# Fewer and larger VectorE instructions around a windowed attention, softmax in PSUM, and one more pair of product tiles added by VectorE

## Chip, cores and metric

One core of one Trainium2 chip. The metric is device time in microseconds of one execution; the time before is the median of three runs.

## The reference

The result mixes a windowed attention `a` and a gated MLP `b` by a gate `g` per row. S = 2048 rows, D = 1024, 32 heads of 32, MLP width 3584. In shortened form:

```python
g = sigmoid((x * gate_w).sum(-1, keepdims=True))
q, k, v = split_heads(x @ wqkv)              # 32 heads of 32
idx = pos[:, None] - arange(8) * 2           # a window of 8 keys, 2 apart
logits = einsum("hsd,hswd->hsw", q, k[idx]) * 32 ** -0.5   # -1e9 where idx < 0
a = einsum("hsw,hswd->hsd", softmax(logits), v[idx]) @ wo
b = (gelu(x @ w_gate) * (x @ w_up)) @ w_down
out = g * a + (1 - g) * b
```

## The kernel before

All data are bf16, sums are in f32 in PSUM. One large SBUF tile, `arena`, holds nearly everything; the constants `R_...` are offsets in KB per partition, and the same place serves several stages in turn. Every large matrix product is done in a Strassen-Winograd form: seven products of halves in place of eight, with sums of weight blocks and of row blocks made beforehand by VectorE.

**The loop.** `x` (transposed) is kept as forms R11 ... T4 for two halves of 1024 rows (s = 0, 1). A `Unit` is two blocks of 128 output columns for one half of the rows: 28 matmuls of 128x128 by 512 (L355), in seven products p1 to p7. Units are q-k tiles (each gives 128 columns of q and the same of k), v tiles, and gate and up tiles of the MLP. The program walks them in the loop at L1342; this text calls one turn of it a **slot**. In slot b the order on TensorE is: p1 of unit b, p73 of unit b-1 (products S3 and S4), p5, then reductions if any are due, p2 and p6 of unit b, p4 of unit b-1. After p73 VectorE does the **join** of unit b-1 (L401): it adds the p5 part to two PSUM banks. p4 of unit b-1 writes one of these banks again. There are 78 units in the walk (slots 2 to 77): 16 q-k, 8 v, and from slot 26 on gate and up.

**The planner.** All other VectorE work is put behind the joins by a planner at build time. It is a list of generators (`bg(gen, prio, wake)`); each yields the cost that it declares for the instruction that it has just issued. `run_bg` is called once at the end of each slot with a credit of 4.7 or 4.8 us (more where reductions were issued) and steps the awake task of the lowest priority number until under 0.3 of the credit is left. `due(n, t)` finishes a task at the start of slot n at the latest. So the declared costs and the credit fix the order of VectorE's instructions, and every engine then runs its own queue in order.

The tasks that matter here:
- `qk_prods` (priority 2): for each q-k tile three products of q with eight shifted copies of k (256 columns each, the fourth block of 256 goes to DRAM for later), as one instruction of 4,096 elements per partition and one of 2,048 (L603 and L596), or three of 2,048. Six product tiles are used in turn, three per q-k tile. For two pairs of tiles (`ADDED`) `qk_add` adds the second tile's products to the first's (L641).
- `qk_reduce` on TensorE (L608): for each product tile four matmuls with a pattern of ones sum over the head's columns, into banks 5 to 7. A pair takes 24 matmuls, an added pair 12.
- `softmax` and `softmax_back`: mask, maximum (L713), subtraction (L715), then the exponential on ScalarE (L723) in a later slot, then sum (L730), reciprocal, gate, and the product into `attn_all` (L735). The exponent's argument `ee` is an f32 area of `arena`, one per call (`R_EX`). From there the weights go to DRAM.
- `spill` (priority 4): the same for the fourth blocks, read back from DRAM; `spill_reduce` uses banks 5 and 6.
- `pv_all` (priority 4.2, then 5): loads weights and v, products (L772) and three levels of folds (L778) for eight blocks. Its last block ends near the end of the loop; its work area lies where the buffer A22 of the down projection will be.
- `sums_pair` (priority 1): four sums of weight blocks per pair of MLP column blocks (L315), one slot after `load_pair` (L170, two DMAs of 512 KB on SP) and before the pair's first unit.
- `h_task` (priority 0): product of gelu(gate) and up (L246), for the last pairs also a scaling with 1 - g (L249), and the store to DRAM by POOL. That of the last pair for s = 0 has priority 5.5 and may run in the slot in which it is made.
- `scale_task`: scalings of loaded h with 1 - g (L943); one of them has priority 6 and runs at the end of the loop.
- `gate_task` (priority 0): the gate's sum, tanh and copies through DRAM, a step per slot.

**Down projection.** `run_last` ends the loop; `down(0)` and `down(1)` follow. They use ten buffers in the arena for h blocks (A11, A12, A21, A22), weights and forms. `pre_down_2` and `pre_down_3` issue the loads of A22, A21, A12 and R21 on SP, in this order; `pre_down_4` has POOL load the last two blocks of A11, A12, A21 and A22 once h's last store for s = 0 has landed. In `down(0)` A11 x R11 and A12 x R21 are plain (L1104); four other products are done in a second Strassen-Winograd level (`level2`, L1071), seven products each, with left and right forms made by VectorE (`forms_L` L1029, `forms_R` L1037) from sums of the buffers (`comb_task` L952).

Of the kernel before, what the change touches and what calls it, by code (L numbers as in the profile page):

```python
# [9 lines left out]
ALU = mybir.AluOpType  # L10
# [26 lines left out]
R_EX = (194.5, 81, 50, 81, 84)  # L37
R_MD = 72
R_ATTN = 73
# [3 lines left out]
R_PROD = 84  # L43
# [25 lines left out]
def kernel(  # L69
# [68 lines left out]
    with tc.manual_schedule(engines={mybir.EngineType.PE, mybir.EngineType.DVE, mybir.EngineType.Activation,  # L138
# [18 lines left out]
        raw = [reg4(R_RAW[i], 2, KT, 2 * P) for i in range(2)]  # L157
        sums = [reg(R_S[i], 4 * 2 * HK * P).rearrange("p (f m k n) -> p f m k n", f=4, m=2, k=HK) for i in range(2)]
# [8 lines left out]
        def load_pair(dst, i):  # L167
            for m, src in ((0, B_w_gate), (1, B_w_up)):
                if i > 1:
                    nc.sync.dma_start(out=dst[:, m, :, :],  # L170
                                      in_=src[:, 2 * P * i:2 * P * (i + 1)].rearrange("(k p) n -> p k n", p=P))
                    continue
                for a in range(2):
                    c0 = (2 * a + i) * P
                    nc.sync.dma_start(out=dst[:, m, :, a * P:(a + 1) * P],
                                      in_=src[:, c0:c0 + P].rearrange("(k p) n -> p k n", p=P))
# [34 lines left out]
        def x_form3(s):  # L211
            f = xf[s]
            TT(out=flat(f.T3), in0=flat(f.R22), in1=flat(f.R12), op=ALU.subtract)
# [70 lines left out]
        def gate_task(s):  # L284
            ts = slice(s * SUP, (s + 1) * SUP)
            zc = small.tile([P, HK, ZI], F32, tag="zc", bufs=2)
            zs = small.tile([P, ZI], F32, tag="zs", bufs=2)
            go = small.tile([P, 2, ZI], BF16, tag="go", bufs=2)
            yield None
            nc.gpsimd.dma_start(out=zc[:], in_=z_d[:, ts].rearrange("g (p i) -> p g i", i=ZI))  # L290
            yield None
            V.tensor_reduce(out=zs[:], in_=zc[:].rearrange("p g i -> p i g"), axis=AX.X, op=ALU.add)
            nc.scalar.activation(out=zs[:], in_=zs[:], func=ACT.Tanh, scale=0.5)
            yield 0.15
            yield None
# [12 lines left out]
            gated.add(s)  # L308

        def sums_pair(w, sm):  # L310
            L11, L12 = w[:, :, 0:HK, 0:P], w[:, :, HK:KT, 0:P]
            L21, L22 = w[:, :, 0:HK, P:2 * P], w[:, :, HK:KT, P:2 * P]
            for o_, a, b_, op in ((sm[:, 0], L21, L22, ALU.add), (sm[:, 1], sm[:, 0], L11, ALU.subtract),
                                  (sm[:, 2], L11, L21, ALU.subtract), (sm[:, 3], L12, sm[:, 1], ALU.subtract)):
                TT(out=o_, in0=a, in1=b_, op=op)  # L315
                yield 0.64

        def gu_forms(w, sm, m):
            r = lambda k0, a: (lambda kt: w[:, m, k0 + kt, a * P:(a + 1) * P])
            z = lambda n: (lambda kt: sm[:, n, m, kt, :])  # L320
            return {"L11": r(0, 0), "L12": r(HK, 0), "L22": r(HK, 1), "S1": z(0), "S2": z(1), "S3": z(2), "S4": z(3)}

        def sums_first(m):
            (L11, L12), (L21, L22) = ((r[:, m, 0:HK, :], r[:, m, HK:KT, :]) for r in raw_ab)
            sm = sums_gu[m]
            for o_, a, b_, op in ((sm[:, 0], L21, L22, ALU.add), (sm[:, 1], sm[:, 0], L11, ALU.subtract),
                                  (sm[:, 2], L11, L21, ALU.subtract), (sm[:, 3], L12, sm[:, 1], ALU.subtract)):
                TT(out=o_, in0=a, in1=b_, op=op)
                yield 0.64
# [124 lines left out]
        def sums_qk(part):  # L454
            L11, L12, L21, L22 = wq
            S1, S2, S4 = sq
            for o_, a, b_, op in (((S1, L21, L22, ALU.add), (S2, S1, L11, ALU.subtract)),
                                  ((L21, L11, L21, ALU.subtract), (S4, L12, S2, ALU.subtract)))[part]:
# [79 lines left out]
        def sums_v():  # L538
            L11, L12 = wv4[:, 0:HK, :, 0:4], wv4[:, HK:KT, :, 0:4]
            L21, L22 = wv4[:, 0:HK, :, 4:8], wv4[:, HK:KT, :, 4:8]  # L540
            for o_, a, b_, op in ((sv[0], L21, L22, ALU.add), (sv[1], sv[0], L11, ALU.subtract),
                                  (sv[2], L12, sv[1], ALU.subtract), (L21, L11, L21, ALU.subtract)):
# [32 lines left out]
        pr_off = [R_PR, R_PR + 4, R_PROD, R_PR + 8, R_PR + 12, R_PROD + 4]  # L575
# [19 lines left out]
        def qk_mult(dst, q, k):  # L595
            TT(out=dst, in0=q.rearrange("p (o s) -> p o s", o=1).to_broadcast([P, NWIN, AC]),  # L596
               in1=_win_ap(k, [[-DIL, NWIN], [1, AC]]), op=ALU.mult)

# [3 lines left out]
        def qk_mult2(dst, q, k, sq, sk):  # L602
            TT(out=dst, in0=_win_ap(q, [[sq, 2], [0, NWIN], [1, AC]]),  # L603
               in1=_win_ap(k, [[sk, 2], [-DIL, NWIN], [1, AC]]), op=ALU.mult)
# [7 lines left out]
        ADDED = {(1, 1), (1, 7)}  # L612
# [3 lines left out]
        def qk_prods(u, s, t):  # L616
# [44 lines left out]
        SPILL = ((((R_PR, R_PR + 4), (R_PR + 8, R_PR + 12)), ((R_PR + 8, R_PR + 12), (R_PROD, R_PROD + 4))),  # L661
                 (((R_PROD, R_PROD + 4), (R_PR + 4, R_PR + 12)), ((R_PR + 4, R_PR + 12), (R_PR, R_PR + 8))))

        def spill(s):
# [3 lines left out]
            for g, (x, y) in enumerate(SPILL[s]):  # L668
                for i, ef in enumerate((x, y)):
                    t = QG * g + 2 * i  # L670
                    if credit[0] > 1.5:
                        qk_mult2(pair_at(*ef), qb[s][:, t, :], kb[s][:, t, HALO:HALO + AC], AC, KV)
                        yield 2.21
                        continue
                    for j in range(2):
                        qk_mult(reg3(ef[j], NWIN, AC), qb[s][:, t + j, :], kb[s][:, t + j, HALO:HALO + AC])
# [24 lines left out]
        def softmax(a, cnt, b0, e):  # L701
            ee = regf(R_EX[e], cnt * SC)
            e4 = ee.rearrange("p (a w s) -> p a w s", a=cnt, w=NWIN)
            sw = ee.rearrange("p (a w s) -> p a s w", a=cnt, w=NWIN)
            lg = banks[:, b0:b0 + cnt, :]
# [568 lines left out]
        def head():  # L1274
            xs, f = xf[0], []
            for i, o in enumerate((R_PROD, R_ATTN)):
# [39 lines left out]
            T(xs.T3, xs.R22, xs.R12)  # L1316
# [83 lines left out]
```

## Time and profile before

| what | us |
|---|---|
| median of the runs (715.04 to 715.99) | 715.1 |
| the profiled execution, its own time | 715.41 |
| its span, first to last instruction | 713.6 |
| TensorE busy | 704.6 |
| VectorE busy | 675.4 |
| ScalarE busy | 329.8 |

The span is 1.8 us shorter than the execution's own time. TensorE's clock was granted at 0.999. The page's first block gives the busy time of each engine (PE is TensorE's matmuls, PEld its weight loads, DVE is VectorE, ACT ScalarE, POOL GpSimd, SP SyncE); its fourth block follows back from the last instruction what released what. In the timeline a line has start, length, engine, source line, operation, output and input, the count of merged instructions, and in brackets the idle time before it with what ended it. The waits view has total, number and longest of the waits in us.

### The profile page before, as it was taken

The page shows a single profiled execution, that of the slowest core. Times are in us where ns is not written, and L with a number is a line of the kernel's source. Part 1 is how long each engine was busy: PE and PEld are TensorE (multiplying, and loading weights), DVE is VectorE, ACT ScalarE, POOL GpSimd, SP SyncE. Part 2 cuts the span into 40 slices and gives each one's busy share as a digit, 9 for nine tenths or more (in the row PEclk, how much of TensorE's full clock was granted, in tenths as well). Part 3 has the DMA queues.
Part 4 walks back from the last instruction along what each step waited for, and adds up shares of the span by engine and source line. Part 5 has one row for each costly group of instructions (what it writes and reads, how often), then busy time and mean ns, then how long its engine had stood idle before and what let it go on. Part 6 is the DMA issues. An engine that isn't in the chain of part 4 may idle for free.

```text
span 713.6 us, 10641 instructions
## 1 busy us (share of the span) xinstructions
PE 704.6 (99%) x4021; PEld 407.4 (57%) x4077; DVE 675.4 (95%) x641; ACT 329.8 (46%) x602; POOL 143.6 (20%) x248
## 2 busy tenths in 40 slices
PE   9999999999999999999999999999999999999998
PEld 4466666655544444444444444444447886758887
DVE  3999999999999999999999999999789999899997
ACT  5554445445557665555555555555322321132431
POOL 1243444115502432221210100101110002100011
PEclk9999999999999999999999999999999999999999
DMA  9989454283375768575662764372981799995951
GB/s 296 326 227 274 153 183 151 85 216 126 118 244 186 234 200 270 163 242 180 216 181 95 273 209 164 114 269 64 393 347 39 305 402 400 421 427 219 386 227 60
DMA packets 94755, 162.03 MB, mean 227 GB/s; under 512 B 23680, under 2 KB 71200, under 8 KB 90352
## 3 DMA queue, kind: packets, MB, share of 16 engines
q1 hardware_dynamic: 77632, 105.46, 43.0%
q0 software_dynamic: 16352, 48.29, 20.0%
q10 hardware_dynamic: 720, 7.60, 2.7%
q8 instruction: 32, 0.52, 0.3%
q14 instruction: 19, 0.16, 0.1%
HBM read 112.17 MB, written 54.14 MB: 233 GB/s over the span
## 4 chain that ended last, share of the span: by engine, by line
PE 96%; DVE 2%; DMA 1%; issue 1%; SPq 0%; ACT 0%; DVEq 0%
PE banks L355 67%; PE banks L1071 19%; PE banks L1104 9%; PE banks L608 2%; DMA arena<-in_B_w_gate_dram 1%; DVE arena L401 0%; DVE arena L943 0%; PE banks L274 0%; DVE arena L772 0%; DVE arena L1285 0%; DVE arena L246 0%; DVE arena L249 0%; DVE arena L223 0%; SPq L144 0%; ACT arena L363 0%
## 5 line engine op out<-in xcount | busy, mean ns | idle before, releaser
L355 PE MATMUL banks<-arena 128*128 128x512 bf16 x2191 | 484.7, 379 | 4.2 <-DVE arena L401 0.9
L355 PEld LDWEIGHTS <-arena 128*128 128x128 bf16 x2240 | 245.7, 110 | 241.4 <-issue 7.7
L1071 PE MATMUL banks<-arena 128*128 128x256 bf16 x1260 | 138.3, 273 | 0.0
L1071 PEld LDWEIGHTS <-arena 128*128 128x128 bf16 x1260 | 123.3, 98 | 15.2 <-issue 0.3
L382 ACT COPY arena<-banks 128x512 f32<-128x512 f32 x80 | 46.9, 586 | 129.7 <-PE banks L355 129.7
L401 DVE TENSOR_TENSOR arena<-banks,arena 128x1024 bf16<-128x1024 f32 x80 | 97.4, 1219 | 4.7 <-PE banks L355 4.0
L363 ACT CAST arena<-banks 128x512 bf16<-128x512 f32 x104 | 60.8, 585 | 42.4 <-PE banks L355 41.1
L772 DVE TENSOR_TENSOR arena<-arena 128x2048 bf16<-128x2048 bf16 (+1 forms) x45 | 74.1, 1670 | 0.4
L778 DVE TENSOR_TENSOR arena<-arena 128x2048 bf16<-128x2048 bf16 (+2 forms) x54 | 68.1, 1261 | 1.0
L252 POOL DMA_DIRECT2D h_d<-arena x28 | 20.3, 730 | 232.8 <-DVE arena L246 154.5
L1104 PE MATMUL banks<-arena 128*128 128x512 bf16 x281 | 62.4, 379 | 0.4
L390 ACT COPY banks<-banks 128x512 f32<-128x512 f32 x80 | 45.6, 570 | 22.3 <-PE banks L355 20.7
L1029 DVE TENSOR_TENSOR arena<-arena 128x2304 bf16<-128x2304 bf16 x40 | 53.3, 1353 | 0.5
L377 ACT COPY banks<-banks 128x512 f32<-128x512 f32 x80 | 46.1, 576 | 14.4 <-PE banks L355 13.3
L1076 ACT COPY banks<-banks 128x256 f32<-128x256 f32 x60 | 21.4, 356 | 59.7 <-PE banks L1071 59.5
L603 DVE TENSOR_TENSOR arena<-arena 128x4096 bf16<-128x4096 bf16 x21 | 47.9, 2284 | 0.3 <-ACT arena L382 0.2
L1104 PEld LDWEIGHTS <-arena 128*128 128x128 bf16 x288 | 28.2, 98 | 33.5
L952 DVE TENSOR_TENSOR arena<-arena 128x2048 bf16<-128x2048 bf16 (+1 forms) x40 | 41.8, 1113 | 3.4 <-DMA arena<-h_d 3.4
L361 ACT ACTIVATE arena<-banks 128x512 bf16<-128x512 f32 x56 | 33.4, 597 | 20.8 <-PE banks L355 20.7
L1037 DVE TENSOR_TENSOR arena<-arena 128x2304 bf16<-128x2304 bf16 x28 | 37.7, 1353 | 0.2
L315 DVE TENSOR_TENSOR arena<-arena 128x1024 bf16<-128x1024 bf16 x56 | 36.1, 686 | 0.5
L246 DVE TENSOR_TENSOR arena<-arena 128x2048 bf16<-128x2048 bf16 x28 | 34.0, 1216 | 2.5 <-ACT arena L363 2.5
(99 smaller groups left out, 459.2 us busy)
## 6 DMA issues: line engine op xcount, KB each, us to landing
arena<-t_d SPq DMA_DIRECT2D x8, 2304.0 KB, 13.4
h_d<-arena POOLq DMA_DIRECT2D x28, 512.0 KB, 4.3
arena<-w_c SPq DMA_DIRECT2D x12, 1152.0 KB, 14.1
t_d<-arena POOLq DMA_DIRECT2D x36, 256.0 KB, 4.4
arena<-h_d SPq DMA_DIRECT2D x6, 1536.0 KB, 12.6
arena<-in_B_w_down_dram SPq DMA_DIRECT2D x28, 256.0 KB, 6.2
r_d<-arena ACTq DMA_DIRECT2D x3, 2304.0 KB, 9.6
arena<-r_d SPq DMA_DIRECT2D x3, 2304.0 KB, 14.3
```

The source lines that it names most:

```text
L355: self.pe = nc.tensor.matmul(ps, lhsT=self.L[form](kt), rhs=rhs[:, kt, :], start=(start and kt == 0), stop=(kt == HK - 1), skip_group_chec ...
L363: nc.scalar.copy(out=o_, in_=i_)
L377: nc.scalar.copy(out=self.Y, in_=self.X)
L382: nc.scalar.copy(out=self.p5s, in_=self.V)
L390: nc.scalar.copy(out=self.Z, in_=self.Y)
L401: TT(out=self.T[:, :, c2s], in0=pair, in1=self.p5s.rearrange("p (o n) -> p o n", o=1).to_broadcast([P, 2, SC]), op=ALU.add)
L603: TT(out=dst, in0=_win_ap(q, [[sq, 2], [0, NWIN], [1, AC]]), in1=_win_ap(k, [[sk, 2], [-DIL, NWIN], [1, AC]]), op=ALU.mult)
L772: TT(out=prod2[:, t % 4:t % 4 + m, :], in0=flat(ab).rearrange("p (o n) -> p o n", o=1).to_broadcast([P, m, NWIN * AC]), in1=_win_ap(v[:, t ...
L778: TT(out=h(0) if w > 1 else o_[:, t:t + m, :], in0=h(0), in1=h(1), op=ALU.add)
L1029: TT(out=o_, in0=a, in1=b_, op=op)
L1071: nc.tensor.matmul(c(i, h, j), lhsT=l[:, kt, j * P:(j + 1) * P], rhs=r[:, kt, :], start=False, stop=(kt == KH - 1), skip_group_check=True)
L1104: nc.tensor.matmul(ps, lhsT=L[:, i, j * P:(j + 1) * P], rhs=R[:, i, :], start=(start and q == 0), stop=(q == NK - 1), skip_group_check=not ...
```

## The change

- `qk_prods` issues one, two or three of a tile's three products as one instruction, as the credit allows (`steps`); `qk_add` likewise. For this the six product tiles lie one behind the other (56 to 80 KB), and `attn_all` and the head's first outputs move.
- `ADDED` gets a third pair, (1, 5).
- `sums_pair` makes S2 and S3 (with its sign turned) by one instruction over two areas; raw weights and sums are laid out for it, and `load_pair` issues a DMA per half of the rows, four in place of two. The sign of S3 and T3 is turned everywhere.
- From the third softmax call on (`e >= 2`) the exponent's argument stays in the PSUM banks in place of the arena.
- `gate_task` waits one more slot between its load and its sum.
- The priority of the last pair's `h_task` for s = 0 goes from 5.5 to 6.5.

The core of the diff:

```diff
-R_EX = (194.5, 81, 50, 81, 84)
-R_MD = 72
-R_ATTN = 73
+R_EX = (194.5, 81)
+R_MD = 80
+R_ATTN = 84
...
+                for h in range(2):
+                    half = src[h * HK * P:(h + 1) * HK * P, :]
+                    if i > 1:
+                        nc.sync.dma_start(out=dst[:, h, m, :, :],
+                                          in_=half[:, 2 * P * i:2 * P * (i + 1)].rearrange("(k p) n -> p k n", p=P))
...
             nc.gpsimd.dma_start(out=zc[:], in_=z_d[:, ts].rearrange("g (p i) -> p g i", i=ZI))
+            yield None
             yield None
...
         def sums_pair(w, sm):
-            L11, L12 = w[:, :, 0:HK, 0:P], w[:, :, HK:KT, 0:P]
-            L21, L22 = w[:, :, 0:HK, P:2 * P], w[:, :, HK:KT, P:2 * P]
-            for o_, a, b_, op in ((sm[:, 0], L21, L22, ALU.add), (sm[:, 1], sm[:, 0], L11, ALU.subtract),
-                                  (sm[:, 2], L11, L21, ALU.subtract), (sm[:, 3], L12, sm[:, 1], ALU.subtract)):
-                TT(out=o_, in0=a, in1=b_, op=op)
-                yield 0.64
+            D2 = [[2 * P, 2 * HK], [1, P]]
+            g = lambda t_, c: _win_ap(t_[:, 0, 0, c * P:c * P + 1], D2)
+            L11, L12, L21, L22 = (g(w[:, h], c) for c in range(2) for h in range(2))
+            S1, S4 = (g(sm[0], c) for c in range(2))
+            S32 = sm[1].rearrange("p f m k n -> p f (m k) n")
+            TT(out=S1, in0=L21, in1=L22, op=ALU.add)
+            yield 0.64
+            TT(out=S32, in0=_win_ap(L21, [[S1.offset - L21.offset, 2]] + D2),
+               in1=_win_ap(L11, [[0, 2]] + D2), op=ALU.subtract)
+            yield 1.14
+            TT(out=S4, in0=L12, in1=S32[:, 1], op=ALU.subtract)
+            yield 0.64
...
-            uu.fin = lambda: bg(h_task(ug.T, uu.T, i, s), *((5.5, now[0]) if (i, s) == (NPAIR - 1, 0) else (7.5 if i == NPAIR - 1 else 0, now[0] + 1)))
+            uu.fin = lambda: bg(h_task(ug.T, uu.T, i, s), *((6.5, now[0]) if (i, s) == (NPAIR - 1, 0) else (7.5 if i == NPAIR - 1 else 0, now[0] + 1)))
...
-        pr_off = [R_PR, R_PR + 4, R_PROD, R_PR + 8, R_PR + 12, R_PROD + 4]
+        pr_off = [R_PR + 4 * k for k in range(6)]
...
+        COST = {1: 1.14, 2: 2.21, 3: 3.28}
+
+        def steps(m):
+            return min(m, 1 + (credit[0] > 1.5) + (credit[0] > 2.6))
+
+        def qk_mult(dst, q, k, m, sq, sk):
+            TT(out=dst, in0=_win_ap(q, [[sq, m], [0, NWIN], [1, AC]]),
+               in1=_win_ap(k, [[sk, m], [-DIL, NWIN], [1, AC]]), op=ALU.mult)
...
-        ADDED = {(1, 1), (1, 7)}
+        ADDED = {(1, 1), (1, 5), (1, 7)}
...
             while a < ND:
-                if a == 0 and credit[0] > 1.5:
-                    qk_mult2(pair_at(pr_off[k], pr_off[k + 1]), u.T[:, 0, 0:AC], u.T[:, 1, 0:AC], AC, AC)
-                    a += 2
-                    yield 2.21
-                else:
-                    qk_mult(out_[a], u.T[:, 0, a * AC:(a + 1) * AC], u.T[:, 1, a * AC:(a + 1) * AC])
-                    a += 1
-                    yield 1.14
+                m = steps(ND - a)
+                qk_mult(run_at(pr_off[k + a], m), u.T[:, 0, a * AC:(a + m) * AC], u.T[:, 1, a * AC:(a + m) * AC], m, AC, AC)
+                a += m
+                yield COST[m]
...
-            for a, b in ((0, 3), (2, 5)):
-                u, v = ((pair_at(pr_off[i], pr_off[i + 1]) if a == 0 else reg(pr_off[i], NWIN * AC)) for i in (a, b))
+            a = 0
+            while a < ND:
+                m = steps(ND - a)
+                u, v = (run_at(pr_off[a + b], m) for b in (0, ND))
                 TT(out=u, in0=u, in1=v, op=ALU.add)
-                yield 2.21 if a == 0 else 1.14
+                a += m
+                yield COST[m]
...
         def softmax(a, cnt, b0, e):
-            ee = regf(R_EX[e], cnt * SC)
+            lg = banks[:, b0:b0 + cnt, :]
+            ee = regf(R_EX[e], cnt * SC) if e < 2 else lg.rearrange("p a n -> p (a n)")
```

More of the change, by code (lines that the diff above doesn't have):

```diff
@@ L42 @@
 R_MASK = 83
-R_PROD = 84
 R_WV = 92
@@ L155 @@
         make_identity(nc, ident[:])
-        raw = [reg4(R_RAW[i], 2, KT, 2 * P) for i in range(2)]
-        sums = [reg(R_S[i], 4 * 2 * HK * P).rearrange("p (f m k n) -> p f m k n", f=4, m=2, k=HK) for i in range(2)]
+        raw = [reg(R_RAW[i], 2 * 2 * HK * 2 * P).rearrange("p (h m k n) -> p h m k n", h=2, m=2, k=HK) for i in range(2)]
+        sums = [(reg4(o, 2, HK, 2 * P), reg(o + 4, 2 * 2 * HK * P).rearrange("p (f m k n) -> p f m k n", f=2, m=2, k=HK)) for o in R_S]
         raw_ab = [reg4(R_W0 + 8 * a, 2, KT, 2 * P) for a in range(2)]
@@ L168, in load_pair @@
             for m, src in ((0, B_w_gate), (1, B_w_up)):
[L169 to L176, printed above, removed]
+                for h in range(2):
[3 more added lines that the diff above has]
+                                          in_=half[:, 2 * P * i:2 * P * (i + 1)].rearrange("(k p) n -> p k n", p=P))
+                        continue
+                    for a in range(2):
+                        c0 = (2 * a + i) * P
+                        nc.sync.dma_start(out=dst[:, h, m, :, a * P:(a + 1) * P],
+                                          in_=half[:, c0:c0 + P].rearrange("(k p) n -> p k n", p=P))
         gwr = small.tile([KT, P], BF16, tag="gwr", bufs=1)
@@ L457, in sums_qk @@
             for o_, a, b_, op in (((S1, L21, L22, ALU.add), (S2, S1, L11, ALU.subtract)),
-                                  ((L21, L11, L21, ALU.subtract), (S4, L12, S2, ALU.subtract)))[part]:
+                                  ((L21, L21, L11, ALU.subtract), (S4, L12, S2, ALU.subtract)))[part]:
                 for hk in range(0, HK, 2):
@@ L659, in spill_load @@
             nc.sync.dma_start(out=kb[s], in_=k_d[s][:])
[L661 to L662 removed]
+        PR_ = pr_off
+        SPILL = ((((PR_[0], PR_[1]), (PR_[2], PR_[3])), ((PR_[2], PR_[3]), (PR_[4], PR_[5]))),
+                 (((PR_[4], PR_[5]), (PR_[1], PR_[3])), ((PR_[1], PR_[3]), (PR_[0], PR_[2]))))
         def spill(s):
@@ L1275, in head @@
             xs, f = xf[0], []
-            for i, o in enumerate((R_PROD, R_ATTN)):
+            for i, o in enumerate((R_PR + 16, R_ATTN)):
                 for m in range(2):
@@ L1315, in head @@
             gate_chunk(1, bank(7))
-            T(xs.T3, xs.R22, xs.R12)
+            T(xs.T3, xs.R12, xs.R22)
             p5(g0)
```

26 lines of the change are left out of this document (11 added, 15 removed).

## The prediction

> **What bounds the kernel now.** I read the page's busy line and chain first, then who makes TensorE wait, then the chain around the one wait, then VectorE's timeline after it.
>
> ```profile
> PE 704.6 (99%) x4021; PEld 407.4 (57%) x4077; DVE 675.4 (95%) x641; ACT 329.8 (46%) x602; POOL 143.6 (20%) x248
> ...
> PE 96%; DVE 2%; DMA 1%; issue 1%; SPq 0%; ACT 0%; DVEq 0%
> ```
>
> TensorE is busy for 704.6 of 713.6 us and is 96% of the chain. Only fewer matmuls, or fewer stalls between them, can shorten the span; but VectorE at 95% can lengthen it.
>
> ```profile
> PE banks L355 <- DVE arena L401: 0.9, 1, 0.9
> ```
> ```profile
> 500.52 0.59 ACT arena L363
> 501.11 0.02 issue
> 501.13 1.24 DVE arena L246
> 502.37 0.02 issue
> 502.39 1.23 DVE arena L249
> 503.62 1.74 DVE arena L943 x2
> 505.35 1.15 DVE arena L401
> ```
>
> The one wait on VectorE that the waits view shows is in slot 77, the last of the loop: VectorE holds h's product of the last pair (L246) until ScalarE has finished its operand at 501.11, then does two scalings (L943), and only then the join (L401) that TensorE needs.
>
> Smaller stalls show in the length of a slot (from a unit's first weight load to the next unit's, L355's rows). Most slots take 6.04 us. Call lag the time from the last matmul of S4 to the start of L401. Slots with a lag of 1.41, 1.45 and 1.59 take 6.14, 6.18 and 6.32; slots with less take 6.04 (unless they hold reductions). So TensorE begins to wait at a lag of 1.31 and from there pays one for one; that is where the matmuls of p4 meet the bank that the join still reads. The lag is never under 0.25. In slots 32 to 76 it runs between 0.25 and 1.59: VectorE has almost nothing to spare there. Such stalls are 0.66 us in all.
>
> Behind the loop VectorE waits for a transfer and then runs without a break until TensorE is close behind it:
>
> ```profile
> 518.74 9.17 DVE L952 TENSOR_TENSOR arena<-arena 128x2048 bf16<-128x2048 bf16 x8
> 531.27 1.29 DVE L952 TENSOR_TENSOR arena<-arena 128x1024 bf16<-128x1024 bf16 x2 [3.36 <-DMA arena<-h_d]
> ```
> ```profile
> 573.50 1.35 DVE L1029 TENSOR_TENSOR arena<-arena 128x2304 bf16<-128x2304 bf16 x1
> 574.76 1.35 DVE L1037 TENSOR_TENSOR arena<-arena 128x2304 bf16<-128x2304 bf16 x1
> ```
> ```profile
> 541.31 55.17 PE banks L1071 x504
> ```
>
> The four level-2 calls take 13.79 us each, seven products of 1.97. The fifth product of the third call starts at 541.31 + 2 x 13.79 + 4 x 1.97 = 576.77 and reads the third right form (L1037), ready at 574.76 + 1.35 = 576.11. Less about 0.1 for the signal, TensorE has 0.55 us in hand there, and the whole row of VectorE work hangs on the tail of A22 that lands at 531.2. The other dependences of these calls have over 1 us.
>
> **The change, part by part.** The planner is deterministic: costs, priorities and wake slots give the order of VectorE's instructions. I followed it by hand for both versions and laid the instructions end to end with the distances of the rows. For the kernel before, this gives the trace's order, and its lags within 0.05 us from slot 31 on; so I use it for the order after.
>
> *Distances.* The page has L596 (2,048 elements) at 1.218, L603 (4,096) at 2.284, L315 (1,024) at 0.686. In the timeline an independent instruction starts 0.083 before the end of the one before it, one that reads its result 0.034 after. So a merge of independent instructions saves 0.07 (1.218 + 2.284 - 0.083 x 2 against 3.35 - 0.083), not the 0.15 that the durations suggest.
>
> *Third pair added.* Slot 19 gets 12 reduction matmuls (L608) in place of 24. Slots with 24 take 7.61 us, with 12 take 6.96: **-0.65 us** of TensorE. VectorE gets one addition over three tiles, 3.35 by L641's size and slope, in slot 18.
>
> *Three products in one.* By the credit (over 2.6) 13 of 16 tiles get one instruction: about 1 us less of VectorE, in slots 4 to 20, where the lag falls back to 0.25 anyway. Worth nothing by itself; if no triple is formed the price is that 1 us, in the same slots.
>
> *Two weight sums in one.* Before: four of 0.684, one of them dependent: 2.52 per pair. After: 0.684, 1.219, 0.684, with both later ones dependent: 2.57. So +0.05 per pair, 0.7 us over 14, and it lies in the tight slots. Bounds for the new instruction, which has an operand repeated by step 0 and one that spans two buffers: 1.2 (L596, which also repeats an operand) to 2.28 if it ran at half rate. I take 1.22, the nearest row, since L603 with the same kind of pattern keeps its rate. Against this, the Trainium skill ("VectorE: DVE Perf Modes", The DRAIN you can't avoid) says that the next operation does not start until the pipe is empty and that the count of operations is what to cut. The trace differs: L401 starts at 497.40 while L943 ends at 497.49. By that rule the merge would gain on every pair, and the sum would be that of the second rival.
>
> *Softmax in PSUM.* The sum over a window (L730) reads SBUF at 2.84 for three blocks and 1.03 for one; the maximum (L713), same shape but from PSUM, takes 1.76 and 0.69. I take those: -1.1 in slot 23 (slack, worth nothing) and -0.34 in each of slots 33 and 37. Bounds: 0 to these. ScalarE's exponential (1.50) stays off the path. The banks are held longer: the first spill reduction writes bank 5 in slot 29, the last read of it is in slot 24, 30 us before; without that cover TensorE would wait up to the 5 us of the softmax's back half.
>
> *Edits at nothing.* Sign flips keep the number of instructions. The loads of a pair become four instead of two (32 more issues, some 0.4 us each on SP, where L170 already waits 171 us in total for TensorE); the sums follow a slot later, about 9 us against a landing of 5; were that lost, each pair would stall for what is missing. Behind them on SP stand only loads for later slots. The later gate step takes away a wait of 1.0 us for zc in slot 4, where the planner leaves credit unused; POOL's copies of the gate come a slot later, needed first in slot 21. Product tile three now lies on the first T set, stored by POOL from 40.98 to 43.3 and landed some 4.4 later; the product starts at about 49, so 1.5 us cover it.
>
> *The tight slots.* The sum of these: the addition of 3.3 us in slots 17 to 21 pushes one pair of spill products and an addition, 3.3 us, behind slot 23. From there to the last fold of the attention (L778), work is 314.8 us before and 3.3 + 0.7 - 0.7 - 0.6 (fewer single products in PV, other dependences) = 2.7 more after. Idle time there falls from 0.56 to 0.13. The lag passes 1.31 in slots 38, 42, 46, 55, 62 (1.85), 64, 67, 70 and a few more: 1.88 us of stalls against 0.71: **+1.17**.
>
> *Priority 6.5.* The scalings now come before h's product, while ScalarE works. In slot 77 the lag is 0.9, not 2.4: **-1.00** (0.89 as a wait, the rest a stretched matmul). So TensorE enters the down projection 0.65 + 1.00 - 1.17 = 0.48 us earlier.
>
> *The transfer.* A22's load may start only when the last fold is done:
>
> ```profile
> SPq L838 <- DVE arena L778: 30.0, 1, 30.0
> ```
>
> That fold ended at 496.36 and now comes 2.28 - 0.65 = 1.63 later; everything behind it on SP (A21, A12, R21, T1, T2) too, and the h store 0.8 later. The windows have 413 and 426 GB/s from 504 to 528, with a DMA share of 1.02: full. Before 502 the packets show some 276 GB/s, so part of the shift is caught up: 276/413 of 1.63 is 1.1. The tail of A22 lands between 0.4 (the h store alone decides) and 1.6 later; I take 1.1. VectorE's row shifts by as much, the right form is ready at 577.2, TensorE would be there at 576.29 and now waits. It leaves 1.1 - 0.55 = **0.5 us later** than before, and what follows is tied to it.
>
> 715.41 (the profiled execution; span 713.6 and 1.8 around it) + 0.5 = 715.9; the median of the three runs is 0.31 under the profiled one, so 715.6.
>
> **Rivals.** (1) *The transfer is not on the path:* VectorE's tail comes as early as before, as the engines had room before 502. Then -0.48 stays: 714.6. Against it: the 3.36 us wait for h_d. (2) *The merge saves:* if each instruction took its whole duration before the next starts, a merged pair would save 2 x 0.686 - 1.219 = 0.15 in place of costing 0.05; the 14 sums take 2.8 us less than I count, the extra stalls go, the fold ends 0.55 earlier than before, the tail about 0.4, and the slack is used up: 714.2. Against it stand the overlapping starts in the rows. The page named above states this rule. (3) *Slower: the merged sum is slow.* It runs in the tight slots, and all that it costs over 1.22 goes to TensorE 14-fold. From 1.32 us on the result passes +1.4; at 2.28 it is +14 (729). For it: an operand that spans two buffers is new; against it: L603's rate. A smaller form of the same: no gain from PSUM, 0.7 us more in slots 33 and 37, 716.3. (4) *The change does not do what it says:* no triples and an addition in pieces; 0.3 us more of VectorE, 715.9.
>
> **How the numbers follow.** My case 0.50 (0 to +1.2), (1) 0.18, (2) 0.12, (3) 0.15, (4) 0.05. 0.2% is 1.43 us, about what a measurement here can tell from no change: below 713.7 or above 716.5. Faster by that needs (2) and the early transfer together, or stalls that all go: 0.13. Slower: (3) and the upper end of my case: 0.24. The rest is the same. The range runs from 714.0, the lower end of (2), to 717.2, my case with the whole shift of the transfer (1.6) and 0.5 us of further stalls.
>
> **What would show it.** Right: 172 matmuls of L608's kind; no wait of 0.9 before slot 77; more slots over 6.04 us between 38 and 73; the last fold over 1 us later; the wait for h_d ending near 532.3; a wait of TensorE of some 1 us near 576. Wrong: merged sums far from 1.22, VectorE idle in slots 38 to 73, or TensorE reaching 576 without a wait.

## The result: 718.7 us, 0.5% slower, and the profile after

The changed kernel takes 718.68 us (median of 5 runs, 718.32 to 719.84) against 715.11 (715.04 to 715.99, 5 runs): a ratio of 1.0051, 95% interval 1.0040 to 1.0063. The forecast was 715.6 with a range to 717.2, so it missed. The profiled execution took 718.47 us with a span of 716.6; before they were 715.41 and 713.6. The clock is granted at 1.0.

The page's busy line, and the waits view for TensorE (total, times, longest):

```profile
PE 707.5 (99%) x4065; PEld 406.3 (57%) x4065; DVE 675.2 (94%) x604; ACT 329.6 (46%) x602; POOL 143.5 (20%) x248
```
```profile
PE banks L364 <- DVE arena L552: 2.5, 1, 2.5
PE banks L1084 <- DVE arena L1050: 0.8, 1, 0.8
...
PE banks L364 <- DVE arena L410: 0.4, 1, 0.4
```

VectorE issues 604 instructions in place of 641 and is busy 675.2 us in place of 675.4. The two totals are alike because gains and losses cancel: by the rows of their lines the products of q and k take 72.3 us in place of 74.5 and the softmaxes' sums 1.8 less, but the additions take 10.1 in place of 7.0, and the weight sums 36.3 in place of 36.1. The wait of 0.9 us for the join in slot 77 is gone; a new one of 2.5 us stands in the loop (L364 is L355 of before, L410 the join), and one of 0.8 in the level-2 calls (L1084 is L1071 of before), as forecast. The timeline of VectorE, then of TensorE, around the new one:

```profile
142.73 1.22 DVE L410 TENSOR_TENSOR arena<-banks,arena 128x1024 bf16<-128x1024 f32 x1
143.87 3.35 DVE L652 TENSOR_TENSOR arena<-arena 128x6144 bf16<-128x6144 bf16 x1
147.13 1.22 DVE L552 TENSOR_TENSOR arena<-arena 128x2048 bf16<-128x2048 bf16 x1
```
```profile
136.23 9.72 PE L364 MATMUL banks<-arena 128*128 128x512 bf16 x44
148.41 1.95 PE L364 MATMUL banks<-arena 128*128 128x512 bf16 x8 [2.46 <-DVE arena L552]
```

L652 is the new addition of the pair (1, 5): three tiles in one instruction. L552 is the last of the four sums of v's weights (`sums_v`, L543 in the kernel before). It writes S3 of v, which p73 of the first v unit reads in slot 19. The addition has priority 2, the sums of v have 2.1, so with the addition in slot 18 the sum comes behind it. TensorE stops for 2.46 us. The same place before, where slot 18 held products of a later tile (L596) and then the sum, which ended at 145.6, in time:

```profile
143.25 1.22 DVE L596 TENSOR_TENSOR arena<-arena 128x2048 bf16<-128x2048 bf16 x1
144.38 1.22 DVE L543 TENSOR_TENSOR arena<-arena 128x2048 bf16<-128x2048 bf16 x1
```

Slot 77 after, the lines that answer to the chain shown of before: the scalings (L956) run first, h's product (L247, L250) behind them, and the join (L410) comes 0.86 after S4's matmuls, not 2.36.

```profile
501.54 2.95 DVE L956 TENSOR_TENSOR arena<-arena,omgrep 128x2048 bf16<-128x2048 bf16 x3
504.41 1.22 DVE L247 TENSOR_TENSOR arena<-arena 128x2048 bf16<-128x2048 bf16 x1
505.66 1.23 DVE L250 TENSOR_TENSOR arena<-arena,omgrep 128x2048 bf16<-128x2048 bf16 x1
506.80 1.22 DVE L410 TENSOR_TENSOR arena<-banks,arena 128x1024 bf16<-128x1024 f32 x1
```

Behind the loop, VectorE's row waits for A22's tail until 534.69 (531.27 before, +3.42), and TensorE for the third right form (timeline, PEld is the weight load):

```profile
534.69 1.29 DVE L965 TENSOR_TENSOR arena<-arena 128x1024 bf16<-128x1024 bf16 x2 [4.87 <-DMA arena<-h_d]
```
```profile
579.58 2.41 PEld L1084 LDWEIGHTS <-arena 128*128 128x128 bf16 x23 [1.12 <-DVE arena L1050]
```

Put together from TensorE's rows, after less before: slots up to 18, -0.3; slot 19, +2.0 (9.6 long in place of 7.6); slots 20 to 76, +1.3; slot 77 and the start of what follows it, -1.1, so that A11 x R11 starts at 511.12 in place of 509.20, +1.9; fifth product of the third level-2 call at 579.58 in place of 576.56, another +1.1. The sum is +3.0, the difference of the spans.

### The profile page after: what moved, and what is told of

Its sections match the earlier page's. It is cut to its first block, busy times and chain, and to the rows that moved or that the text cites. A ratio compares the mean times of both kernels' runs of the same rounds, so it can differ in the third digit from the quotient of the medians.

```text
span 716.6 us, 10688 instructions
## 1 busy us (share of the span) xinstructions
PE 707.5 (99%) x4065; PEld 406.3 (57%) x4065; DVE 675.2 (94%) x604; ACT 329.6 (46%) x602; POOL 143.5 (20%) x248
## 5 line engine op out<-in xcount | busy, mean ns | idle before, releaser
L364 PE MATMUL banks<-arena 128*128 128x512 bf16 x2240 | 488.6, 379 | 3.5 <-DVE arena L552 2.5
L364 PEld LDWEIGHTS <-arena 128*128 128x128 bf16 x2240 | 245.7, 110 | 244.2 <-issue 8.0
L1084 PE MATMUL banks<-arena 128*128 128x256 bf16 x1260 | 138.5, 273 | 0.8 <-DVE arena L1050 0.8
L1084 PEld LDWEIGHTS <-arena 128*128 128x128 bf16 x1260 | 123.2, 98 | 16.3 <-DVE arena L1050 1.1
L410 DVE TENSOR_TENSOR arena<-banks,arena 128x1024 bf16<-128x1024 f32 x80 | 97.4, 1218 | 9.6 <-ACT arena L418 3.4
L785 DVE TENSOR_TENSOR arena<-arena 128x4096 bf16<-128x4096 bf16 (+1 forms) x38 | 73.4, 1950 | 0.4
L616 DVE TENSOR_TENSOR arena<-arena 128x6144 bf16<-128x6144 bf16 (+2 forms) x28 | 72.0, 2587 | 0.6 <-PE banks L621 0.6
L965 DVE TENSOR_TENSOR arena<-arena 128x2048 bf16<-128x2048 bf16 (+1 forms) x40 | 41.8, 1110 | 4.9 <-DMA arena<-h_d 4.9
L247 DVE TENSOR_TENSOR arena<-arena 128x2048 bf16<-128x2048 bf16 x28 | 33.9, 1215 | 0.0
L1122 POOL DMA_DIRECT2D out_dram<-arena x19 | 10.3, 542 | 102.6 <-DVE arena L1126 74.6
```

The lines of the kernel that those rows point to most:

```text
L364: self.pe = nc.tensor.matmul(ps, lhsT=self.L[form](kt), rhs=rhs[:, kt, :], start=(start and kt == 0), stop=(kt == HK - 1), skip_group_chec ...
L410: TT(out=self.T[:, :, c2s], in0=pair, in1=self.p5s.rearrange("p (o n) -> p o n", o=1).to_broadcast([P, 2, SC]), op=ALU.add)
L616: TT(out=dst, in0=_win_ap(q, [[sq, m], [0, NWIN], [1, AC]]), in1=_win_ap(k, [[sk, m], [-DIL, NWIN], [1, AC]]), op=ALU.mult)
L785: TT(out=prod2[:, t % 4:t % 4 + m, :], in0=flat(ab).rearrange("p (o n) -> p o n", o=1).to_broadcast([P, m, NWIN * AC]), in1=_win_ap(v[:, t ...
L965: TT(out=f(o_), in0=f(a), in1=f(b), op=op)
L1084: nc.tensor.matmul(c(i, h, j), lhsT=l[:, kt, j * P:(j + 1) * P], rhs=r[:, kt, :], start=False, stop=(kt == KH - 1), skip_group_check=True)
```

## Experiments

Line numbers can differ by up to three from those of the changed kernel, as lines come in or go. The kernel before was run beside each on the same chip; its median is given with the result. Stalls are added up as in the prediction: what the lags of the slots (from the rows of the last S4 weight load and of the join) have over 1.31.

**The fourth sum of v ahead of the addition.** The changed kernel with

```diff
+        at(Q0 + 2 * NT, lambda: (setattr(sv_task, "prio", 1.9), tasks.sort(key=lambda t_: t_.prio)))
         due(Q0 + 2 * NT + 1, sv_task)
```

> The changed kernel, with the fourth sum of v's weights put ahead of the added pair's addition in slot 18. Theory V (the loss is that sum: it came behind the third pair's addition of 3.35 us, and TensorE waited 2.5 us for it): the wait on the v sum is gone, slot 77 starts 0.5 us later than before instead of 3.0, A22's load leaves 1.6 us later than before instead of 4.1, total 715.9 (+0.8). Rival L (the loss is VectorE's load in the loop, and the wait for the v sum only takes the place of others): 717.5 to 718.5.

Measured: 716.03 (714.84 to 718.00) against 715.34, ratio 1.0012 (1.0001 to 1.0023). VectorE's timeline has the two instructions in the other order, TensorE waits for neither, and slot 19 is 7.0 long:

```profile
144.08 1.22 DVE L552 TENSOR_TENSOR arena<-arena 128x2048 bf16<-128x2048 bf16 x1
145.22 3.35 DVE L652 TENSOR_TENSOR arena<-arena 128x6144 bf16<-128x6144 bf16 x1
```

So 2.7 of the 3.6 us lost (718.68 - 716.03 of 718.68 - 715.11; 2.9 if each is taken against the kernel before beside it) hang on the place of one instruction of 1.2 us. Three of the ten runs took 717.75 to 718.00; the profiled one took 715.62, so no profile shows those. A22's load is issued at 498.01, 1.63 after that of before: the shift of the forecast. TensorE's wait near 576 stays (0.6 in the waits view).

**No third pair.** The changed kernel with `ADDED = {(1, 1), (1, 7)}`.

> The changed kernel with two added pairs in place of three. Theory V: no wait for the v sum, since no addition stands ahead of it; 0.65 us of reductions come back; the walk gives 2.6 us of stalls in the loop, TensorE enters the down projection 0.9 us later than before, the last fold 4 us earlier, so no wait near 576: 716.0 (+0.9). Rival L (the other parts cost the time): 718 or more.

Measured: 715.68 (715.60 to 717.19) against 715.34, ratio 1.0009 (1.0000 to 1.0018). The long wait is gone with the addition. But the stalls of slots 24 to 76 are 2.44 us, not the 0.66 of before; the third pair is therefore not what makes the slots tight.

**The merged weight sum taken apart,** with three pairs and the sum of v in its place. The first experiment with, in `sums_pair`,

```diff
-            TT(out=S32, in0=_win_ap(L21, [[S1.offset - L21.offset, 2]] + D2),
-               in1=_win_ap(L11, [[0, 2]] + D2), op=ALU.subtract)
-            yield 1.14
+            S3, S2 = S32[:, 0], S32[:, 1]
+            TT(out=S2, in0=S1, in1=L11, op=ALU.subtract)
+            yield 0.64
+            TT(out=S3, in0=L21, in1=L11, op=ALU.subtract)
+            yield 0.64
```

> The kernel of the run before this, with the merged weight sum taken apart into two instructions (four per pair, declared 0.64 each, as before). By the walk through the planner TensorE's stalls in the loop fall from 1.9 to 0.7 us and it enters the down projection 1.6 us earlier than in the kernel before; but the last fold comes 4.3 us later, and with it A22's load. Theory T (behind the loop the landing of A22's tail decides): TensorE waits some 4 us at the fifth product of the third level-2 call, 718.1 (+3.0). Rival (the transfers are not on the path): 713.5 (-1.6).

Measured: 719.10 (718.91 to 719.50) against 715.34, ratio 1.0051 (1.0035 to 1.0068). The stalls do fall, from 1.95 to 0.70, and A11 x R11 starts at 507.19, 2.0 earlier than before. All of it, and more, is lost behind the loop. TensorE stops at a place that I had not named, ahead of the last two blocks of A11 x R11, whose data are the tail of A11 (the 78 matmuls of the row are the rest of this product and A12 x R21):

```profile
525.83 18.91 PE L1120 MATMUL banks<-arena 128*128 128x512 bf16 x78 [3.79 <-DMA arena<-h_d]
```

POOL may load the tails of the blocks only when the last store of h has landed. That store is issued at 507.29 (504.14 before) and lands at 517.22 (511.67); the last fold is late too (A22's load at 500.40, against 498.01 in the first experiment). A11's tail, the first of the four, lands 8.3 us after its issue, at 525.78, and TensorE is there at 522.04. Before, the tail landed at 519.71 and TensorE came at 524.0, with 4.3 us in hand. Not all of the loss is the wait: behind it the clock is granted at 0.57 of full from 526 to 530 (1.00 before and after), and TensorE, which is 2.2 later than before at this tail, is 3.6 later at the first level-2 call.

**T2 out of the tails' way.** The first experiment with T2's load given to ScalarE's queue behind the first copy of A12 x R21:

```diff
-            loads(0, "T1", "T2")
+            loads(0, "T1")
...
+                if not last and j == 0:
+                    nc.scalar.dma_start(out=B["T2"], in_=t_d[1][:])
```

> The kernel with the v sum first, and the load of T2 (2.3 MB, needed only some 20 us later) issued by ScalarE after the first copy of A12 x R21 in place of ahead of the tails. Theory T: the tails land some 4 us earlier, no wait at the fifth product of the third level-2 call, and TensorE keeps the 0.5 us by which it enters the down projection earlier: 714.6 (-0.5). Rival (the tail's landing is not on the path): as with the v sum first alone, 715.9.

Measured: 715.00 (714.40 to 715.45) against 715.34, ratio 0.9995 (0.9985 to 1.0004). A22's load and its tail are issued as in the first experiment (498.29 and 514.92 against 498.01 and 515.01), but the tail lands at 527.40 in place of 531.86. VectorE's wait for h and TensorE's near 576 are gone. The mean share of the DMA engines was 1.02 from 504 to 528 before: what T2 moves there, the tails lack (this reading is argued; the landing is measured).

**These three edits together.**

> All three edits together: the fourth sum of v ahead of the addition, the merged weight sum taken apart, T2's load behind the first copy of A12 x R21. The walk over VectorE's order says that TensorE enters the down projection 1.63 us earlier than in the kernel before (the third pair, the priority and the undone stalls all at TensorE's disposal), while the last fold, and with it A22's load, comes 4.3 us later. Theory T (only the transfer stands in the way, and T2 is 4.5 of its 18 KB a partition): T2 out of the way gives back about 4 us, as e3_t2_late showed no wait on A22 with a fold 1.6 later, so most of the 1.63 is kept: 713.5 to 714.3 where the kernel before has 715.3. Rival (the store of the last pair of h and the first reads of A are now late themselves): TensorE waits 2 to 3 us on a load of h at the head of the level-2 work, and the time is 716 to 717.

Measured: 717.98 (715.87 to 720.65, the widest spread of all) against 715.17, ratio 1.0036 (1.0022 to 1.0049). The rival's wait is there: the waits view has `L1120 <- DMA arena<-h_d` with 3.1 us, as A11's tail lands at 525.30. The time is above the 716 to 717 that it gave, and the clock goes with a part of that: it is granted at 0.50 from 525 to 528, behind that wait, and the four runs with a mean clock of 1.0 take 715.87 to 717.29, the six with 0.995 to 0.998 take 717.76 to 720.65. T2's place did not help here: the store of h ahead of the tails is itself late (issued at 507.48), and A11's tail still lands 8.8 us after its issue.

**Two pairs, four sums.** The changed kernel with products and additions issued as in the kernel before (two in one instruction where the credit allows, then one: 21 of 4,096 elements and 22 of 2,048, the counts of before; the expectations call this one product to an instruction), four sums (as above), `ADDED = {(1, 1), (1, 7)}` and T2's load moved. Softmaxes in PSUM and the priority stay, and so do the smaller edits.

> Two added pairs as in the kernel before, (1,1) and (1,7), one product to an instruction and four sums to a pair of weights; kept are the softmaxes in PSUM and the priority 6.5, and T2's load stands behind the first copy of A12 x R21. By the walk VectorE has 3.3 us less to do than with three pairs: TensorE enters the down projection 1.31 us earlier than in the kernel before and the last fold ends 0.3 us earlier. If the parts add up as the walk says, 715.3 - 1.3 = 714.0 or a little less. Rival (the softmax in PSUM and the priority give nothing, all of e3_t2_late's gain is T2's): 715.0 or more.

Measured: 713.87 (713.64 to 714.96) against 715.17, ratio 0.9982 (0.9973 to 0.9991): as the walk has it, and faster than both kernels. The same with T2's load in its place:

> The kernel of e6_two_pairs with T2's load back in its place ahead of the tails. Theory T: TensorE enters the down projection 1.3 us earlier, the fold and A22's load only 0.3 earlier, so at the fifth product of the third level-2 call 0.55 + 0.3 of the 1.3 are kept and the rest is waited for: 714.4, with a wait of about 0.4 us near 575. Rival (T2's place matters only where the fold is late): 713.9, as e6_two_pairs.

Measured: 714.02 (713.72 to 714.91) against 715.09, ratio 0.9988 (0.9978 to 0.9997). No wait shows near 575; the tail of A22 lands at 529.82, 1.35 earlier than before. So the rival fits: with T2 in either place the gain is about the same (the intervals overlap), and T2's place showed an effect only where fold and store are late. What is left of the change here, softmaxes in PSUM, priority and the smaller edits, brings some 1.1 us.

**The priority alone.** The kernel before with 6.5 in place of 5.5.

> The kernel before with the one priority changed, 5.5 to 6.5: the two scalings go ahead of h's product of the last pair. The wait of 0.9 us ahead of the join in slot 77 must vanish, and TensorE enters the down projection 1.0 us earlier. Theory T (the fifth product of the third level-2 call had 0.55 us in hand on VectorE's row, which hangs on A22's tail): 0.55 of it is kept, 714.7. Rival (the transfer is not what VectorE's row hangs on): the whole 1.0 is kept, 714.3. If the store of the last pair of h, which this edit puts later, is on the path, nothing or less than nothing is left: 715.3 or more.

Measured: 714.78 (713.95 to 715.12) against 715.17, ratio 0.9988 (0.9979 to 0.9998). The wait ahead of the join is gone. By the interval the gain lies between 0.1 and 1.5 us, which holds both theories. The profile leans to T: A11 x R11 starts 0.74 earlier than before (508.46), but the span is only 0.3 shorter, and the waits view has 0.2 us for the third right form (L1071 <- L1037). By the rows that form had 0.40 us in hand (worked out below), and VectorE's row starts 0.12 later here (531.39), which leaves the 0.3.

**The other two pairs.** Four sums, products and additions issued as in the kernel before, `ADDED = {(1, 1), (1, 5)}`; then the same with the fourth sum of v first.

> Two added pairs, but (1,1) and (1,5) instead of (1,1) and (1,7), one product to an instruction and four sums; T2 stays in its place. The pair (1,7) is then reduced by TensorE in slots where VectorE would otherwise add late. By the walk TensorE enters the down projection 1.02 us earlier than in the kernel before and the last fold ends 5.0 us earlier, so the tail of A22 is out of the way: 715.3 - 1.0 = 714.3. In slot 18 the fourth sum of v stands behind the addition as in the changed kernel; the walk has VectorE less loaded there and puts the wait under 0.5 us. Rival (the wait of 2.5 us is there whatever the load): 716.5.

> The kernel of e7_pairs_1_5 with the fourth sum of v ahead of the addition, the edit of e1_v_first. If the wait of 2.9 us ahead of the first v unit is all that e7_pairs_1_5 lost, it goes, TensorE enters the down projection 1.0 us earlier than in the kernel before with a fold 5 us earlier: 714.2, some 4 under e7_pairs_1_5 (its wait, and 0.5 to 1 for the places that come right). Rival (the addition in slot 18 delays the products of the next slot whatever stands before it): 716 or more, with a wait in slot 18 or 19 that names another instruction.

Measured: without the edit 718.61 (717.82 to 719.29) against 715.17, ratio 1.0044 (1.0029 to 1.0059), with a wait of 2.9 us for the sum of v; my walk had missed it. With the edit 714.60 (714.00 to 715.17) against 715.09, ratio 0.9991 (0.9981 to 1.0000), and slot 19 takes 7.0 us in place of 11.6. VectorE has a whole addition less to do here than in the changed kernel, and the wait is there all the same: it is the place of the addition in slot 18 that counts, not VectorE's load.

```profile
PE banks L366 <- DVE arena L554: 2.9, 1, 2.9
```

The wait explains 2.9 of the 4.7 by which slot 19 is longer. The rest is the clock. These rows of the run without the edit have a stretch, its length, the busy time of each engine with its count of instructions, the granted clock, the DMA share and GB/s:

```profile
144.00:148.00 4.00, 1.79 (x9) 0.90 (x7) 4.00 (x4) 1.73 (x3) 0.38 (x1) 1.00 0.44 155
148.00:152.00 4.00, 3.33 (x8) 1.27 (x9) 0.61 (x1) 0.00 (x0) 0.00 (x0) 0.57 1.18 304
152.00:156.00 4.00, 3.95 (x27) 2.00 (x27) 3.59 (x3) 1.45 (x3) 0.54 (x1) 1.00 1.28 215
```

When TensorE goes on at 148.67, its first eight matmuls start 0.43 us apart and not 0.22, which is 1.7 us more. In the profiled execution of the changed kernel, where the wait was 2.46, they start 0.22 apart at once and the clock stays at 1.00.

**The merged sum by itself.** The kernel with two pairs and T2 moved, with S2 and S3 in one instruction again; and the same with its declared cost set to that of the two that it replaces:

```diff
-            yield 1.14
+            yield 1.28
```

> The kernel of e6_two_pairs with two of a pair's weight sums in one instruction again, and nothing else changed. The theory of the prediction (a merged sum saves no time, as the next instruction may start 0.083 us before the end of an independent one but only 0.034 after the end of one that it reads): VectorE's stretch per pair grows by 0.05, and the walk over the planner, which now gives out three steps in place of four, has the stalls of slots 32 to 76 grow from 0.4 to 2.4 us: e6_two_pairs + 2.0, 715.9 where the kernel before has 715.2. If only the 0.05 a pair counts and not the changed order: 714.6 at most. Rival (instructions wait for the end of the one before, so a merge saves 0.15 a pair, 2.1 us of VectorE): 713.9 or less.

> The kernel of e9_merged_two with one number changed: the merged weight sum is declared to the planner at 1.28, the sum of the two that it replaces, in place of 1.14. The instructions are the same; only their order may change. Theory D (the merged sum itself costs 0.05 a pair; the rest of e9_merged_two's 2.2 us comes from the 0.14 a pair that the planner believes saved, with which it puts one more step ahead of a join and issues pairs of products of p x v one by one): by the walk the stalls of slots 32 to 76 fall from 2.4 to 0.7 us, and the time is 714.1 to 714.5 where the kernel before has 715.1. Rival (the merged sum's reads and writes hold up the join themselves): 716, as e9_merged_two.

Measured: merged at 1.14, 716.15 (715.79 to 716.50) against 715.09, ratio 1.0013 (1.0003 to 1.0022); merged at 1.28, 714.37 (714.13 to 714.67) against 715.25, ratio 0.9987 (0.9977 to 0.9997). The stalls of slots 24 to 76 are 0.39 us with four sums, 2.66 merged at 1.14, and 0.72 merged at 1.28. VectorE's timeline shows how, in the stretch ahead of a join. Four sums:

```profile
305.01 0.68 DVE L318 TENSOR_TENSOR arena<-arena 128x1024 bf16<-128x1024 bf16 x1
305.72 0.69 DVE L321 TENSOR_TENSOR arena<-arena 128x1024 bf16<-128x1024 bf16 x1
306.33 0.68 DVE L323 TENSOR_TENSOR arena<-arena 128x1024 bf16<-128x1024 bf16 x1
306.94 0.68 DVE L325 TENSOR_TENSOR arena<-arena 128x1024 bf16<-128x1024 bf16 x1
307.54 1.95 DVE L793 TENSOR_TENSOR arena<-arena 128x2048 bf16<-128x2048 bf16 x2
309.40 1.22 DVE L412 TENSOR_TENSOR arena<-banks,arena 128x1024 bf16<-128x1024 f32 x1
310.54 1.21 DVE L247 TENSOR_TENSOR arena<-arena 128x2048 bf16<-128x2048 bf16 x1
311.67 2.28 DVE L787 TENSOR_TENSOR arena<-arena 128x4096 bf16<-128x4096 bf16 x1
```

Merged, at 1.14 (the same place, which this run reaches 0.07 earlier):

```profile
304.94 0.68 DVE L318 TENSOR_TENSOR arena<-arena 128x1024 bf16<-128x1024 bf16 x1
305.65 1.23 DVE L320 TENSOR_TENSOR arena<-arena 128x2048 bf16<-128x2048 bf16 x1
306.91 0.69 DVE L323 TENSOR_TENSOR arena<-arena 128x1024 bf16<-128x1024 bf16 x1
307.52 1.95 DVE L791 TENSOR_TENSOR arena<-arena 128x2048 bf16<-128x2048 bf16 x2
309.50 1.23 DVE L785 TENSOR_TENSOR arena<-arena 128x2048 bf16<-128x2048 bf16 x1
310.64 1.22 DVE L410 TENSOR_TENSOR arena<-banks,arena 128x1024 bf16<-128x1024 f32 x1
311.78 1.22 DVE L247 TENSOR_TENSOR arena<-arena 128x2048 bf16<-128x2048 bf16 x1
312.91 1.22 DVE L785 TENSOR_TENSOR arena<-arena 128x2048 bf16<-128x2048 bf16 x1
```

From the first sum to the next work it is 307.54 - 305.01 = 2.53 apart and 307.52 - 304.94 = 2.58 merged: the +0.05 of the forecast. But the planner counts 0.64 + 1.14 + 0.64 = 2.42 where it counted 2.56. With the 0.14 it fits one more product of p x v (L785, L787 in the other kernel) ahead of the join, which comes 1.2 later; that product is now issued alone, where with four sums the two are one instruction of 2.28 behind the join. At 1.28 the two come as one behind the join again.

## Why the prediction was wrong

**The step that failed** is the sentence on the third pair: "VectorE gets one addition over three tiles, 3.35, in slot 18". Size and slot are right (3.35 at 143.87), and so is what it saves (slot 19 takes 7.0 in place of 7.6 once nothing waits). What is missing is who is queued behind it on VectorE, and who waits for that: the fourth sum of v, and p73 of the first v unit one slot later. The walk was held against the trace of the kernel before alone, and its lags from slot 31 on; slot 18 of the changed kernel is in neither. The price is 2.67 us in slot 19 (9.6 against the 6.96 of the text). Before, that sum started at 144.38; after, at 147.13. None of the rivals named this; the nearest slower one, a slow merged sum, is refuted by its row, 1.225 us.

**The rest of the sum held in size.** With that sum of v moved, the median is 716.03, inside the range and 0.4 from the forecast, though three of its ten runs lie above the range. Term by term, in the changed kernel: reductions -0.65, as forecast (7.61 to 6.96, seen in slot 19 once nothing waits); tight slots +1.17 forecast, +1.3 measured; priority -1.00 and -1.1 (lag 0.86 for 0.9); behind the loop 0.98 lost by the forecast (from -0.48 to +0.5), 1.1 measured.

**The cause of the tight slots was wrong.** The text gives them to "the addition of 3.3 us" pushed behind slot 23. With three pairs and four sums the stalls are 0.70, with two pairs and merged sums 2.44: they come from the merge. The merge was priced as 0.05 a pair, from the distances of the rows; its real price, some 2 us where two pairs are added, lies in the cost that it declares to the planner. With three pairs, taking the merge apart costs more behind the loop than it saves in the slots (719.10 against 716.03). The walk over the planner contained this, and I put its result down to the wrong edit.

**The transfer was on the path, as forecast,** and harder than forecast. The last fold comes 4.14 later in the changed kernel (A22's load at 500.52 against 496.38), since the wait of slot 19 pushes everything behind it, and the tail 3.42 later: 0.83 of the shift, where I had taken 1.1/1.63 = 0.67. The third right form had less in hand than the 0.55 of the text: TensorE came to it at 576.56, not 576.77, the form was ready at 576.11, and after the change the weight load starts 0.05 behind it (579.53, 579.58), so 0.40. Of 3.42 that leaves 3.0, and the span is 3.0 longer. What the loop itself lost, +1.9 at the start of A11 x R11, lies below that and is covered by it. Rival (1), the transfer not on the path, falls with T2's experiment, which keeps the fold and moves only the tail, and takes the wait away.

**The rest of the change** went as costed. 13 instructions of three tiles (6,144 elements) in `qk_prods`, as counted, and the three additions came whole, so rival (4) falls; what the triples bring by themselves was not measured. Sums in PSUM take 1.749 for three blocks and 0.683 for one, where the row of before had 2.84 and 1.03. Rival (2), that the merge saves, falls with 2.58 against 2.53 above. The Trainium skill ("VectorE: DVE Perf Modes", The DRAIN you can't avoid) states both that the next operation waits for the pipe to be empty and that one which is not held starts earlier; the rows here follow the second: the sums at 306.33 and 306.94 each start before the one ahead of them has ended, while 305.72 and 306.91, which read the result ahead of them, start after its end.

**What stays open:** why the spread of some kernels is so wide. For three edits together (715.87 to 720.65) it goes in part with the granted clock, as shown above; of the changed kernel's own five runs the three at a clock of 1.0 take 718.32 to 718.68, the two at 0.998 both 719.84. But the first experiment spreads from 714.84 to 718.00 with 0.999 or 1.0 in every run, and that is not explained. Open is also how much each of PSUM softmax and priority brings; they were only timed together with the smaller edits (some 1.1 us), and the priority by itself (0.1 to 1.5).

## What to carry to other kernels

When an operation is put into an engine's queue, look for what now stands behind it and when that is due: an addition of 3.35 us that was affordable in sum cost 2.7 us because one sum of 1.22 with a due time lay behind it. Where a planner orders work by declared costs, a merged operation must declare what it takes and not what it should save: 0.14 us too little, 14 times, cost 1.9 us (1.06 above the kernel before beside it, against 0.88 below). And a gain for the engine at the front is worth only what the next bound leaves: here the store of h and the fold that frees A22's place, whose lateness can eat 2 us of earlier matmuls and more. A long stop of TensorE can cost more than the stop itself: look at the granted clock behind it before the whole loss is put down to the wait.

## What the runs showed of the hardware

- Independent VectorE sums of 0.684 us started 0.61 us apart. An instruction of twice the size takes 1.225; the next one started 1.14 behind its start where it was independent (309.50 to 310.64) and 1.26 where it read the result (305.65 to 306.91). So two small ones in one save some 0.08 if no dependence is added, an estimate from these rows; the merge of the weight sums added one and lost 0.05.
- A sum over f32 data by stride took 2.84 us from SBUF and 1.749 from PSUM for 128x1536, 1.03 and 0.683 for 128x512: I knew the price for the maximum alone and had only carried it over.
- With the DMA engines full (mean share 1.02), one load of 2.3 MB moved away brought the landing of another queue's 256 KB forward by 4.5 us (531.86 to 527.40) with all issues within 0.3 us of where they were. The Trainium skill ("DMA: Bandwidth & Descriptors", Queues, rings and completion order) says that an engine goes round between the queues that have work; the landing agrees with two queues sharing an engine, though no view here shows its turns.
- After TensorE had stood still for 2.9, 3.1 and 3.8 us (the pairs (1, 1) and (1, 5), three edits together, four sums), the clock was granted at about half for a short while: 0.57 on average over 4 us in the first and the last, which is 3.4 us at half speed. That cost 1.2 to 1.7 us on top of the wait in the three profiles. After 2.46 us it did not happen in the one profile at hand; where the limit lies was not measured.
